# A decayed-state attention with a mixture-of-experts layer on one core: state update in one piece per head, wide scores, placed element-wise work and a new order

## The chip, the cores and the metric

The kernel runs on one NeuronCore of a Trainium2 chip. The metric is the device time of one execution in microseconds (us). The core has a TensorE for matmuls (PE; its weight loads are shown as PEld), a VectorE (DVE), a ScalarE (ACT), a GpSimd (POOL) and a SyncE (SP), which issues the DMA transfers.

## The reference

Four batches, eight heads, 768 steps, head size 48. Each step multiplies a complex state by a decay, adds the outer product of key and value, and reads it with the query. The result `x` (768 x 384 per batch) goes through four experts of attention, of which the two best are mixed per token.

```python
scale = np.minimum(mag, 0.999) / (mag + 1e-06)     # mag = |a|
for t in range(S):
    new_re = ar * S_re - ai * S_im
    new_im = ar * S_im + ai * S_re
    kv = np.einsum('bhd,bhe->bhde', k[:, :, t], v[:, :, t])
    S_re, S_im = (new_re + kv, new_im)
    y[:, :, t] = np.einsum('bhd,bhde->bhe', q[:, :, t], S_re)
...
for e in range(E):
    scores = scale * (q @ k.transpose(0, 2, 1))    # q, k, v = x @ wq[e], x @ wk[e], x @ wv[e]
    ...
    ye = a @ v @ wo[e]                             # a: causal softmax of scores
    for kk in range(K):
        mask = topk[:, :, kk] == e
        out += mask[..., None] * w[:, :, kk:kk + 1] * ye
```

## The kernel before, in words

The recurrence is worked in six chunks of 128 steps per batch. *Preparation* (`logs`, `atan`, `angles`, `sincos`, `products`) turns the decays `ab` into running magnitudes and angles and multiplies them into queries and keys (`qk`), on tiles of 128 x 768, in batch 0 in three pieces of 128 x 256. `regroup` copies these by DMA into `fm`, where each head has 96 rows (real and imaginary parts of 48).

Per chunk follow three steps. `head` transposes the keys to `kts` (bank `pk`), and makes the score product `psc` of 128 x 128 per head, which a mask turns into `pts`. It is issued in two groups of four heads; each head's 128 key columns are split into two halves of 64. `state` makes `pu`, the update of the state of 96 x 48 per head, out of `kts` and the values `vt`; the 96 rows are split into 64 and 32. VectorE adds the old state (`wst1`) and multiplies by the chunk's decay (`tst`). The last chunk of a batch has no update. `tail` adds, for each pair of heads, the product of `pts` with the values and that of the old state with the queries into `yu`, which is split into a high part `xh` and a rest `xl`.

The expert layer then projects (`proj`, bank `pp`; `vproj`, `pv`), finds row maxima (`maxpass`, `pm`), and works attention in two pairs of experts: `score` (`pss`, exponential into `pe`), `av` (`po`), `norm` (sums `dn`, weights `cb`) and `wo` (`pw`, out to `ob`). In `av` the exponentials of the later key chunks are added into the first one's tile (`SUMS`), so that `norm` needs only a few matmuls for the sums: 16 such additions per batch.

All operations are first recorded in a list (`record`), one entry per step with its engine. `ENG0` and `ENG` say for some kinds of work whether VectorE (`d`) or GpSimd (`p`) does it; the additions into `pe` (kind `sum`) and the key products stand on `p`, the other kinds on `d`. `ORDER` is a written-out order of the whole list; each engine runs its own entries in that order. `ROOMS` says which buffer each tile takes. `FILL` puts a number of dummy matmuls on the mask `keep` ahead of an entry (line 744); everything else is issued at line 752, so almost all rows of the profile carry L752 and are told apart by their tiles. Tables for ScalarE's functions are loaded at line 750.

Of the kernel before, what the change touches and what calls it, by code (L numbers as in the profile page):

```python
# [807 lines left out]
```

## Time and profile before

| what | us |
|---|---|
| median of 3 runs (526.93 to 715.49) | 529.76 |
| the profiled execution | 527.1 |
| its span, first to last instruction | 525.4 |

The profile is of one execution. An fp32 matmul shows as two records, and two weight loads. A group's busy time is the union of its records, so that for matmuls, which are pipelined, it is less than count times mean; how long a stream of them takes is read from the starts in the timeline. Waits are idle time of an engine before an instruction, with the engine that ended it.

### The profile page before, as it was taken

How to read it: one execution, taken by the hardware profiler on the slowest of the kernel's cores; microseconds unless marked ns; L12 is line 12 of the kernel's file. 1: busy time of each engine (PE TensorE's matmuls, PEld its weight loads, DVE VectorE, ACT ScalarE, POOL GpSimd, SP SyncE). 2: the span in 40 equal slices, each digit the busy share in tenths (PEclk: the TensorE clock that was granted, in tenths of full speed). 3: DMA queues.
4: the chain of work that ended last, by engine and by line, in shares of the span. 5: the costliest groups of instructions: out<-in, count | busy, mean ns of one | idle time of the engine just before them, and what ended most of it. 6: DMA issues, size and time to landing. Idle time of an engine off the chain costs nothing.

```text
span 525.4 us, 11296 instructions
## 1 busy us (share of the span) xinstructions
PE 485.1 (92%) x4546; PEld 364.4 (69%) x4546; DVE 350.0 (67%) x706; ACT 302.4 (58%) x532; POOL 179.1 (34%) x192
## 2 busy tenths in 40 slices
PE   8979999988799999999889997999899999998986
PEld 3437676766467777787567785887677878887655
DVE  4887868798964469699953686789944232647521
ACT  7897777696533777475613794856632233134453
POOL 1315050413440526341431643720425030040782
PEclk9979999989899989999997997999999998999999
DMA  8561728152370820615342702325620401010002
GB/s 294 185 201 32 207 50 257 53 171 69 88 181 18 226 85 17 200 47 153 100 141 58 210 1 75 87 72 148 181 65 21 118 2 55 17 46 30 17 1 92
DMA packets 29717, 53.52 MB, mean 102 GB/s; under 512 B 3936, under 2 KB 11616, under 8 KB 29664
## 3 DMA queue, kind: packets, MB, share of 16 engines
q1 hardware_dynamic: 29664, 52.79, 34.5%
q8 instruction: 36, 0.59, 0.5%
q14 instruction: 17, 0.14, 0.1%
HBM read 26.74 MB, written 4.72 MB: 60 GB/s over the span
## 4 chain that ended last, share of the span: by engine, by line
PE 56%; DVE 19%; ACT 13%; issue 5%; POOL 3%; DMA 3%; SPq 1%; POOLq 0%; DVEq 0%; ACTq 0%
PE pu L752 13%; PE pp L752 6%; PE psc L752 6%; PE yu L752 5%; PE pss L752 4%; DVE qk L752 4%; PE po L752 4%; DVE ab L752 4%; ACT qk L752 3%; PE pw L752 3%; PE pv L752 3%; POOL pe L752 2%; DVE junk L752 2%; ACT ab L752 2%; ACT L750 2%
## 5 line engine op out<-in xcount | busy, mean ns | idle before, releaser
L752 POOL TENSOR_TENSOR pe<-pe 128x512 f32<-128x512 f32 (+2 forms) x64 | 82.0, 1284 | 100.4 <-PE po L752 77.7
L752 PE MATMUL pu<-vt,kts 128*32 128x48 f32 (+1 forms) x640 | 75.0, 233 | 3.6 <-DVE xl L752 2.9
L752 PEld LDWEIGHTS pu<-vt,kts 128*32 128x32 f32 (+1 forms) x640 | 54.7, 125 | 24.1 <-DVE xl L752 3.4
L752 ACT ACTIVATE pe<-pss 128x512 f32<-128x512 f32 (+3 forms) x80 | 47.3, 616 | 37.9 <-PE pss L752 32.5
L752 POOL TENSOR_TENSOR qk<-qk,ab 128x256 f32<-128x256 f32 (+1 forms) x36 | 49.1, 1366 | 41.4 <-ACT ab L752 19.9
L752 PE MATMUL psc<-fm 96*64 96x128 f32 x768 | 52.3, 283 | 4.5 <-ACT kts L752 1.9
L752 PE MATMUL pss<-qka 64*128 64x256 f32 (+3 forms) x480 | 50.2, 319 | 6.2 <-ACT pe L752 4.5
L752 PEld LDWEIGHTS psc<-fm 96*64 96x64 f32 x768 | 43.0, 139 | 11.7 <-issue 2.2
L750 ACT ACT_TABLE_LOAD x39 | 50.0, 1283 | 1.4 <-PEq L797 0.8
L752 ACT ACTIVATE qk<-qk 128x256 f32<-128x256 f32 (+1 forms) x72 | 44.9, 629 | 7.5 <-DVE qk L752 6.6
L752 PEld LDWEIGHTS pss<-qka 64*128 64x128 f32 x480 | 35.6, 190 | 18.4 <-ACT pe L752 7.4
L752 POOL TENSOR_TENSOR qk<-qk 128x256 f32<-128x256 f32 (+1 forms) x18 | 20.8, 1158 | 74.1 <-ACT qk L752 45.0
L744 PEld LDWEIGHTS <-keep 128*128 128x128 bf16 x222 | 22.2, 103 | 34.0 <-issue 11.6
L752 PE MATMUL po<-pe,v 128*64 128x256 f32 (+3 forms) x320 | 45.0, 403 | 0.0
L752 POOL TENSOR_SCALAR_AFFINE_SELECT pe<-pe 128x256 f32<-128x256 f32 x48 | 22.4, 473 | 63.5 <-ACT pe L752 63.4
L752 DVE TENSOR_TENSOR pts<-psc,keep 128x512 f32<-128x512 f32 x48 | 32.5, 686 | 15.9 <-PE psc L752 15.7
L752 DVE CUSTOM_DVE_ANT_0 junk<-pm,negm 128x128 bf16<-128x128 f32 (+3 forms) x64 | 31.1, 486 | 15.7 <-PE pm L752 14.8
L752 PE MATMUL yu<-pts,vt 128*64 128x128 f32 x384 | 38.2, 288 | 1.8 <-DVE pts L752 1.0
L752 ACT ACTIVATE ab<-ab 128x256 f32<-128x256 f32 (+1 forms) x54 | 33.1, 625 | 11.5 <-DVE ab L752 11.3
L744 PE MATMUL psc<-keep 128*128 128x512 bf16 x125 | 31.1, 413 | 4.2 <-ACT kts L752 2.3
L752 ACT ACTIVATE r<-dn,col 128x512 f32<-128x512 f32 (+1 forms) x16 | 9.3, 582 | 43.8 <-PE dn L752 43.8
L752 DVE TENSOR_TENSOR qk<-qk,ab 128x256 f32<-128x256 f32 (+1 forms) x36 | 29.7, 827 | 5.3 <-ACT ab L752 4.7
(113 smaller groups left out, 987.6 us busy)
## 6 DMA issues: line engine op xcount, KB each, us to landing
fm<-qk SPq DMA_DIRECT2D x72, 192.8 KB, 3.6
qk<-in_ak_dram SPq DMA_DIRECT2D x12, 768.0 KB, 6.0
ab<-in_ak_dram SPq DMA_DIRECT2D x18, 384.0 KB, 5.2
vt<-in_vk_dram SPq DMA_DIRECT2D x12, 512.0 KB, 4.4
out_dram<-ob SPq DMA_DIRECT2D x24, 192.0 KB, 1.9
fm<-qk SPq DMA_DIRECT2D x24, 128.5 KB, 3.7
ab<-in_ak_dram SPq DMA_DIRECT2D x9, 256.0 KB, 3.6
wst<-in_w_dram SPq DMA_DIRECT2D x3, 514.0 KB, 9.3
```

What stands on the lines that cost most here:

```text
L744: nc.tensor.matmul(z, real(plan.busy), real(plan.busy)[:, None, :].to_broadcast([128, 4, 128]), start=True, stop=True)
L750: nc.scalar.preload_act_table_set(need)
L752: getattr(getattr(nc, engine), name)(*map(real, a), **{n: real(x) for n, x in k.items()})
```

## The change

- `state`: one matmul of 96 columns of weights per head, where there were one of 64 and one of 32.
- `head`: one matmul of 128 columns of weights per head, where there were two of 64.
- `tail`: three entries instead of one: the products of the first `pts`, those of the second, then all products of the state.
- Placement: `ENG0`, `ENG` and `eng` go; most element-wise work stands on VectorE or ScalarE by default, and a table `HOME` moves single entries to VectorE or GpSimd. `moved` writes an ACT entry in another engine's form. By it, of the 64 additions into `pe`, 24 stay on GpSimd and 40 go to VectorE; 52 copies and casts out of ScalarE's list go to VectorE (`xh` 10, `kts` 10, `lg` 10, `v` 7, `qka` 6, `ob` 6, `ot` 3); of the 36 scalings and absolute values of the angles, 12 stay on VectorE, 2 go to GpSimd and 22 to ScalarE; the multiplications with the decay go to GpSimd in 7 of 20 updates; and of the products in preparation GpSimd has 35 of 768 columns (27 before) and 11 of 256 (27 before).
- `logs`: the copy of the chunk ends' decay (`E`), on GpSimd before, is an ACT copy that `HOME` moves to VectorE 5 times and to GpSimd 3 times.
- `ORDER`, `ROOMS` and `FILL` are new; the dummy matmuls are 172 instead of 222.

```diff
-SUMS = ((1, 2, 3), (1, 2, 3, 4, 5))
-
-FILL = {297: 113, 299: 9, 330: 33, 363: 3, 384: 10, 409: 3, 428: 2, 437: 10, 451: 14, 465: 1, 502: 12, 504: 3, 638: 5, 966: 2, 2003: 2}
...
+HOME = {39: 'vector',
+ 47: 'vector',
...
+FILL = {293: 4, 299: 118, 301: 2, 315: 10, 318: 7, 439: 12, 462: 16, 513: 2, 2047: 1}
...
-        p.mul(eng("ratio", b, j, k0), Bi, Bi, A)
-        if eng("square", b, j, k0) == V:
-            p.act(A, Bi, AF.Square)
-        else:
-            p.mul(G, A, Bi, Bi)
+        p.mul(V, Bi, Bi, A)
+        p.act(A, Bi, AF.Square)
...
-        p.ts(eng("turns", b, j, k0), Bi, A, 0.5 / math.pi, MAGIC, OP.mult, OP.add)
+        p.act(Bi, A, AF.Copy, scale=0.5 / math.pi, bias=MAGIC)
...
-            p.mm(*((q[64 * a:64 * a + 64, i], part(b, c, 4 * g + i, 1)[:, 64 * a:64 * a + 64], part(b, c, 4 * g + i, 0), True, True)
-                   for i in range(4) for a in range(2)))
+            p.mm(*((q[:, i], part(b, c, 4 * g + i, 1), part(b, c, 4 * g + i, 0), True, True) for i in range(4)))
...
-        p.mm(*((pu[64 * a:64 * a + (64, 32)[a], h], kt[b, c][:, h, 64 * a:64 * a + (64, 32)[a]], v[:, c % 2, h, :D], True, True)
-               for h in range(H) for a in range(2)))
+        p.mm(*((pu[:, h], kt[b, c][:, h], v[:, c % 2, h, :D], True, True) for h in range(H)))
...
-            p.mul(eng("decay", 1, c, b) if b else V, t, x, e)
+            p.mul(V, t, x, e)
...
-        calls = []
-        for g in range(4):
-            for i in range(2):
-                calls.append((yu[64 * i:64 * i + 64, g], v[:, c % 2, 2 * g + i], pt[b, c, g // 2][:, 2 * (g % 2) + i], True, c == 0))
-            if c:
-                for i in range(2):
-                    calls.append((yu[64 * i:64 * i + D, g], st[b, c][:, 2 * g + i], part(b, c, 2 * g + i, 0), False, True))
-        p.mm(*calls)
+        for g in range(0, 4, 2):
+            p.mm(*((yu[64 * i:64 * i + 64, g + x], v[:, c % 2, 2 * (g + x) + i], pt[b, c, g // 2][:, 2 * x + i], c == 0 or g + x == 0, c == 0)
+                   for x in range(2) for i in range(2)))
+        if c:
+            p.mm(*((yu[64 * i:64 * i + D, g], st[b, c][:, 2 * g + i], part(b, c, 2 * g + i, 0), False, g == 3)
+                   for g in range(4) for i in range(2)))
...
-            if i in SUMS[g]:
+            if i in SUMS[b][pr][g]:
...
-                p.tt(eng("sum", 1, i, 0), y, y, x, OP.add)
+                p.tt(V, y, y, x, OP.add)
...
+def moved(engine, name, a, k):
+
+    if name != "activation":
+        return engine, name, a, k
+    o, x, f = a
+    if f == AF.Square:
+        return engine, "tensor_tensor", (o, x, x), dict(op=OP.mult)
+    if f == AF.Abs:
+        return engine, "tensor_scalar", (o.bitcast(I32), x.bitcast(I32), 0x7FFFFFFF, None), dict(op0=OP.bitwise_and, op1=OP.bypass)
+    if k:
+        return engine, "tensor_scalar", (o, x, k["scale"], k["bias"]), dict(op0=OP.mult, op1=OP.add)
+    return engine, "tensor_copy", (o, x), k
...
+            if i in HOME and HOME[i] != engine:
+                engine, name, a, k = moved(HOME[i], name, a, k)
```

TensorE's list before, at the tail of batch 0's second chunk and its state update (sizes are rows x columns of the result; the update goes on in this pattern for eight heads):

```order
L752 MATMUL psc<-fm 64x128 x8
L752 MATMUL pk<-ident,fm 128x96 x4
L752 MATMUL yu<-pts,vt 64x128 x2
L752 MATMUL yu<-fm,tst 48x128 x2
L752 MATMUL yu<-pts,vt 64x128 x2
L752 MATMUL yu<-fm,tst 48x128 x2
L752 MATMUL yu<-pts,vt 64x128 x2
L752 MATMUL yu<-fm,tst 48x128 x2
L752 MATMUL yu<-pts,vt 64x128 x2
L752 MATMUL yu<-fm,tst 48x128 x2
L752 MATMUL pu<-vt,kts 64x48
L752 MATMUL pu<-vt,kts 32x48
```

The same list of the changed kernel, some chunks of batch 0 later (`pm` is the row maximum of the expert layer):

```order
L904 MATMUL pk<-ident,fm 128x96 x4
L904 MATMUL pu<-vt,kts 96x48 x8
L904 MATMUL psc<-fm 128x128 x4
L904 MATMUL yu<-pts,vt 64x128 x8
L904 MATMUL yu<-fm,tst 48x128 x8
L904 MATMUL psc<-fm 128x128 x4
L904 MATMUL pm<-qka 128x256 x2
L904 MATMUL pu<-vt,kts 96x48 x8
L904 MATMUL yu<-pts,vt 64x128 x8
L904 MATMUL yu<-fm,tst 48x128 x8
```

An update is now eight equal matmuls of 96 rows, half a chunk's scores are four of 128, and the tail has its `pts` products together and its state products behind them; other work stands between the two halves of the scores.

GpSimd's list before, at the end of the program (additions into `pe`, and AFFINE_SELECT, the causal mask on it):

```order
L752 AFFINE_SELECT pe<-pe 128x2x128
L752 AFFINE_SELECT pe<-pe 128x256
L752 TENSOR_TENSOR pe<-pe 128x2x384
L752 TENSOR_TENSOR pe<-pe 128x2x128
L752 AFFINE_SELECT pe<-pe 128x2x128
L752 TENSOR_TENSOR pe<-pe 128x2x256
L752 TENSOR_TENSOR pe<-pe 128x512 x3
L752 AFFINE_SELECT pe<-pe 128x2x128
L752 TENSOR_TENSOR pe<-pe 128x512
L752 AFFINE_SELECT pe<-pe 128x256
L752 TENSOR_TENSOR pe<-pe 128x2x128
```

The end of VectorE's list in the changed kernel (`r` and `ot` are the normalised result and its split):

```order
L904 TENSOR_TENSOR pe<-pe 128x2x384
L904 TENSOR_TENSOR pe<-pe 128x2x128
L904 TENSOR_TENSOR pe<-pe 128x2x256
L904 TENSOR_TENSOR r<-r,cb 128x256
L904 TENSOR_TENSOR r<-r,po 128x256
L904 TENSOR_TENSOR r<-r,cb 128x512
L904 TENSOR_TENSOR r<-r,po 128x512
L904 TENSOR_TENSOR pe<-pe 128x512
L904 TENSOR_TENSOR ot_5085<-r,ot_5085 128x512
L904 TENSOR_TENSOR pe<-pe 128x512 x3
```

Of the last batch's 16 additions 14 moved from GpSimd's list to VectorE's, where they stand among the normalisation's products; two, one of 512 and one of 256, stay on GpSimd.

## Rows read from the trace of the kernel before

**Rows 1.** The head of the page and its part 1, busy time by engine.

```profile
span 525.4 us, 11296 instructions
...
PE 485.1 (92%) x4546; PEld 364.4 (69%) x4546; DVE 350.0 (67%) x706; ACT 302.4 (58%) x532; POOL 179.1 (34%) x192
```

**Rows 2.** Part 4 of the page, the chain that ended last.

```profile
PE 56%; DVE 19%; ACT 13%; issue 5%; POOL 3%; DMA 3%; SPq 1%; POOLq 0%; DVEq 0%; ACTq 0%
PE pu L752 13%; PE pp L752 6%; PE psc L752 6%; PE yu L752 5%; PE pss L752 4%; DVE qk L752 4%; PE po L752 4%; DVE ab L752 4%; ACT qk L752 3%; PE pw L752 3%; PE pv L752 3%; POOL pe L752 2%; DVE junk L752 2%; ACT ab L752 2%; ACT L750 2%
```

**Rows 3.** TensorE groups with shapes kept apart; then count | busy us, mean ns.

```profile
L752 PE MATMUL pu<-vt,kts 128*64 128x48 f32 x320 | 51.3, 243 | 3.6 <-DVE xl L752 2.9 <-ACT kts L752 0.6
...
L752 PE MATMUL pu<-vt,kts 128*32 128x48 f32 x320 | 44.8, 223 | 0.0
```

**Rows 4.** TensorE's timeline, 190 to 215: start us, length us, engine, line, records.

```profile
196.08 1.97 PE L752 MATMUL psc<-fm 96*64 96x128 f32 x32
197.88 3.60 PE L752 MATMUL pu<-vt,kts 128*64 128x48 f32 x32
201.41 0.87 PE L752 MATMUL po<-pe,v 128*64 128x384 f32 x4
...
209.16 0.52 PE L752 MATMUL pp<-xh,wlo 128*128 128x256 f32 x3
209.52 0.53 PE L752 MATMUL pp<-xl,whi 128*128 128x256 f32 x3
209.89 0.52 PE L752 MATMUL pp<-xh,whi 128*128 128x256 f32 x3
```

**Rows 5.** Weight loads by shape (rows*columns of the array).

```profile
L752 PEld LDWEIGHTS pu<-vt,kts 128*64 128x64 f32 x320 | 32.2, 139 | 15.0 <-DVE xl L752 3.4 <-ACT kts L752 1.3 <-issue 0.2
...
L752 PEld LDWEIGHTS pu<-vt,kts 128*32 128x32 f32 x320 | 22.5, 110 | 9.0
...
L752 PEld LDWEIGHTS pp<-xh,whi 128*128 128x128 f32 x144 | 20.4, 189 | 3.2 <-issue 1.0 <-ACT kts L752 0.7 <-DMA xh<-xh 0.3
```

**Rows 6.** A piece of the chain by time; loads of the dummies (page).

```profile
52.74 7.23 PE pv L744 x33
...
L744 PEld LDWEIGHTS <-keep 128*128 128x128 bf16 x222 | 22.2, 103 | 34.0 <-issue 11.6
```

**Rows 7.** Groups by shape on POOL, DVE and ACT.

```profile
L752 POOL TENSOR_TENSOR pe<-pe 128x512 f32<-128x512 f32 x40 | 53.2, 1334 | 89.6 <-PE po L752 68.1 <-ACT pe L752 19.4
...
L752 DVE TENSOR_TENSOR qk<-qk,ab 128x768 f32<-128x768 f32 x18 | 20.1, 1115 | 0.3
...
L752 POOL TENSOR_TENSOR pe<-pe 128x768 f32<-128x768 f32 x8 | 14.9, 1859 | 9.5 <-PE po L752 9.5
...
L752 ACT ACTIVATE xh<-yu 128x512 fp32r<-128x512 f32 x24 | 14.3, 596 | 28.9 <-PE yu L752 28.9
...
L752 POOL TENSOR_TENSOR pe<-pe 128x256 f32<-128x256 f32 x16 | 13.9, 872 | 1.2
...
L752 DVE TENSOR_TENSOR qk<-qk,ab 128x256 f32<-128x256 f32 x18 | 9.6, 539 | 5.0 <-ACT ab L752 4.7
...
L752 DVE TENSOR_SCALAR ab<-ab 128x768 f32<-128x768 f32 x9 | 5.2, 573 | 0.1
```

**Rows 8.** Stretches: from:to, length, busy PE, PEld, DVE, ACT, POOL (x instructions), clock.

```profile
100.00:150.00 50.00, 41.97 (x335) 30.02 (x331) 45.90 (x84) 33.11 (x49) 18.18 (x14) 0.93 0.37 104
...
484.00:517.00 33.00, 29.30 (x278) 19.36 (x276) 11.56 (x24) 17.16 (x32) 24.32 (x28) 1.00 0.06 20
```

**Rows 9.** First and last of seven POOL pieces of the chain, 488 to 515.

```profile
488.73 1.84 POOL pe L752
...
513.14 1.65 POOL pe L752 x2
```

**Rows 10.** Span and mean granted TensorE clock.

```profile
core 0: 525.4 us, clock 0.963
```

More of the change, by code (lines that the diff above doesn't have):

```diff
@@ L66 @@
-ROOMS = {'ab': [0, 1, 0, 1, 0, 1, 0, 1, 0, 1, 0, 1],
- 'carry': [0, 3, 4, 3, 5, 2],
- 'fm': [1, 0, 1, 0, 1, 0, 1, 0, 1, 0, 1, 0],
+SUMS = ((((1, 2, 3), (1, 2, 3, 4, 5)), ((1, 2, 3), (1, 2, 3, 4, 5))), (((1, 2, 3), (1, 2, 3, 4, 5)), ((1, 2, 3), (1, 2, 3, 4, 5))),
+ (((1, 2, 3), (1, 2, 3, 4, 5)), ((1, 2, 3), (1, 2, 3, 4, 5))), (((1, 2, 3), (1, 2, 3, 4, 5)), ((1, 2, 3), (1, 2, 3, 4, 5))))
+HOME = {39: 'vector',
+ 47: 'vector',
+ 54: 'vector',
+ 62: 'vector',
+ 69: 'vector',
+ 77: 'vector',
+ 86: 'vector',
+ 88: 'vector',
+ 91: 'vector',
+ 93: 'vector',
+ 96: 'vector',
+ 146: 'vector',
+ 147: 'gpsimd',
+ 161: 'gpsimd',
+ 170: 'vector',
+ 177: 'vector',
+ 180: 'vector',
+ 182: 'vector',
+ 191: 'gpsimd',
+ 193: 'gpsimd',
+ 196: 'gpsimd',
+ 199: 'gpsimd',
+ 218: 'gpsimd',
+ 233: 'gpsimd',
+ 255: 'vector',
+ 261: 'gpsimd',
+ 271: 'gpsimd',
+ 279: 'gpsimd',
+ 280: 'gpsimd',
+ 281: 'gpsimd',
+ 334: 'vector',
+ 372: 'gpsimd',
+ 388: 'gpsimd',
+ 392: 'vector',
+ 409: 'vector',
+ 443: 'gpsimd',
+ 470: 'vector',
+ 526: 'gpsimd',
+ 540: 'vector',
+ 541: 'gpsimd',
+ 554: 'gpsimd',
+ 556: 'gpsimd',
+ 564: 'gpsimd',
+ 574: 'gpsimd',
+ 590: 'gpsimd',
+ 618: 'gpsimd',
+ 626: 'gpsimd',
+ 628: 'gpsimd',
+ 636: 'gpsimd',
+ 653: 'vector',
+ 674: 'gpsimd',
+ 677: 'gpsimd',
+ 682: 'gpsimd',
+ 705: 'gpsimd',
+ 713: 'gpsimd',
+ 715: 'gpsimd',
+ 722: 'gpsimd',
+ 733: 'vector',
+ 734: 'gpsimd',
+ 736: 'gpsimd',
+ 744: 'gpsimd',
+ 747: 'gpsimd',
+ 760: 'vector',
+ 762: 'vector',
+ 783: 'gpsimd',
+ 787: 'vector',
+ 800: 'vector',
+ 801: 'vector',
+ 803: 'vector',
+ 804: 'vector',
+ 829: 'vector',
+ 831: 'vector',
+ 845: 'vector',
+ 854: 'gpsimd',
+ 871: 'vector',
+ 875: 'vector',
+ 900: 'vector',
+ 909: 'gpsimd',
+ 929: 'vector',
+ 932: 'vector',
+ 938: 'vector',
+ 992: 'gpsimd',
+ 1030: 'gpsimd',
+ 1039: 'vector',
+ 1069: 'gpsimd',
+ 1082: 'gpsimd',
+ 1092: 'gpsimd',
+ 1094: 'gpsimd',
+ 1102: 'gpsimd',
+ 1113: 'vector',
+ 1116: 'vector',
+ 1138: 'gpsimd',
+ 1140: 'gpsimd',
+ 1143: 'vector',
+ 1151: 'gpsimd',
+ 1157: 'gpsimd',
+ 1169: 'gpsimd',
+ 1180: 'gpsimd',
+ 1181: 'gpsimd',
+ 1182: 'gpsimd',
+ 1188: 'gpsimd',
+ 1199: 'gpsimd',
+ 1200: 'gpsimd',
+ 1202: 'gpsimd',
+ 1210: 'gpsimd',
+ 1211: 'gpsimd',
+ 1213: 'gpsimd',
+ 1228: 'vector',
+ 1237: 'vector',
+ 1253: 'vector',
+ 1308: 'vector',
+ 1313: 'vector',
+ 1320: 'gpsimd',
+ 1331: 'vector',
+ 1388: 'vector',
+ 1402: 'vector',
+ 1458: 'gpsimd',
+ 1473: 'gpsimd',
+ 1480: 'gpsimd',
+ 1486: 'gpsimd',
+ 1488: 'gpsimd',
+ 1496: 'gpsimd',
+ 1522: 'gpsimd',
+ 1527: 'gpsimd',
+ 1558: 'gpsimd',
+ 1560: 'gpsimd',
+ 1568: 'gpsimd',
+ 1579: 'vector',
+ 1582: 'vector',
+ 1585: 'vector',
+ 1593: 'vector',
+ 1604: 'gpsimd',
+ 1606: 'gpsimd',
+ 1609: 'vector',
+ 1623: 'gpsimd',
+ 1634: 'gpsimd',
+ 1635: 'gpsimd',
+ 1637: 'gpsimd',
+ 1645: 'gpsimd',
+ 1646: 'gpsimd',
+ 1647: 'gpsimd',
+ 1648: 'gpsimd',
+ 1666: 'gpsimd',
+ 1668: 'gpsimd',
+ 1676: 'gpsimd',
+ 1677: 'gpsimd',
+ 1678: 'gpsimd',
+ 1679: 'gpsimd',
+ 1703: 'vector',
+ 1719: 'vector',
+ 1726: 'vector',
+ 1729: 'vector',
+ 1733: 'vector',
+ 1774: 'vector',
+ 1779: 'vector',
+ 1790: 'vector',
+ 1797: 'vector',
+ 1806: 'vector',
+ 1807: 'vector',
+ 1832: 'vector',
+ 1868: 'vector',
+ 1870: 'vector',
+ 1871: 'vector',
+ 1954: 'gpsimd',
+ 1972: 'gpsimd',
+ 2026: 'gpsimd',
+ 2033: 'vector'}
@@ L69 @@
+FILL = {293: 4, 299: 118, 301: 2, 315: 10, 318: 7, 439: 12, 462: 16, 513: 2, 2047: 1}
+ROOMS = {'ab': [1, 0, 1, 0, 1, 0, 0, 1, 0, 0, 1, 0],
+ 'carry': [5, 2, 3, 0, 1, 3],
+ 'fm': [1, 0, 1, 1, 0, 1, 1, 0, 1, 0, 1, 0],
  'gcf': [0, 0, 0, 0],
@@ L384, in logs @@
         p.act(Y, X, AF.Exp)
-        p.put(G, "tensor_copy", E.rearrange("p x k c -> p k x c"),
-              Y.rearrange("p k (c t) -> p k c t", t=C)[:, :, None, :, C - 1].to_broadcast([128, k1 - k0, 2, 2]))
-        p.mul(eng("exp_q", b, j, k0), Q, Q, Y)
+        p.copy(E.rearrange("p x k c -> p k x c"),
+               Y.rearrange("p k (c t) -> p k c t", t=C)[:, :, None, :, C - 1].to_broadcast([128, k1 - k0, 2, 2]))
+        p.mul(V, Q, Q, Y)
         p.act(X, X, AF.Exp, scale=-1.0)
-        p.mul(eng("exp_k", b, j, k0), K, K, X)
+        p.mul(V, K, K, X)
     def atan(b, j, k0, k1):
@@ L415, in products @@
         A, Bi, Af, Bf, Q, K, X, Y, E = views(b, j, k0, k1)
[L416 to L419 removed]
+        p.mul(V, X, Q, Af)
+        p.mul(V, Y, K, Af)
+        p.mul(V, Q, Q, Bf)
+        p.mul(V, K, K, Bf)
     def regroup(b, k, js=(0, 1, 2)):
@@ L632, in norm @@
         dn = p.bank("dn")[:, :n]
-        left = [i for u in UNITS[g] for i in u if i not in SUMS[g]]
+        left = [i for u in UNITS[g] for i in u if i not in SUMS[b][pr][g]]
         p.mm(*((dn[64 * e:64 * e + 64, cols(g, i)[0] - t0:], onecols, pe[b, pr, g, i][:, e],
@@ L746, in attention_moe @@
         for engine, name, a, k in plan.ops[i]:
+            a, k = [real(x) for x in a], {n: real(x) for n, x in k.items()}
+            if i in HOME and HOME[i] != engine:
+                engine, name, a, k = moved(HOME[i], name, a, k)
             if name == "activation":
@@ L751, in attention_moe @@
                     table = need
-            getattr(getattr(nc, engine), name)(*map(real, a), **{n: real(x) for n, x in k.items()})
+            getattr(getattr(nc, engine), name)(*a, **k)
     last = {}
```

56 lines of the change are left out of this document (12 added, 44 removed), and 180 rows, old and new, of tables (ORDER, ROOMS).

## The prediction

> **What bounds the kernel now.** I read the busy shares first. TensorE is busy 485.1 us of a span of 525.4, VectorE 350.0, ScalarE 302.4, GpSimd 179.1 [rows 1]. A busy TensorE need not be the bound, so the chain that ended last came next: 56% of it is TensorE, 19% VectorE, 13% ScalarE, and its largest single item is the state update, `pu`, with 13% of the span, some 69 us [rows 2]. There are 20 state updates (four batches, five chunks each; the last chunk has none), so nearly every one stands on the chain at its full length. What happens in one of them is seen in TensorE's timeline: 32 records of `pu` begin at 197.88 and the next work, `po`, begins at 201.41, so eight heads take 3.53 us, 441 ns a head [rows 4]. A head has four records (each fp32 matmul shows as two), 64 columns of weights twice and 32 columns twice, with only 48 columns streaming. Beside it stands the score product: 32 records from 196.08 to 197.88, 225 ns a head for four records with 128 columns streaming [rows 4]. Work with almost three times the columns takes half the time. What differs is that the scores always alternate between two halves of 64 columns, while `pu` alternates between a width of 64 and one of 32, 320 records of each [rows 3]. So `pu` isn't paid by its columns; it is paid by changing the array's shape twice a head.
>
> **The change, part by part.**
>
> *State update in one piece.* 160 pairs of pieces (64 and 32 columns) become 160 matmuls of 96, so 640 records become 320, and no change of shape is left inside an update. The trace of before has no fp32 matmul of full width with plain weights, so I bound the cost of a record. Below: the streaming alone. The scores show 225/2 = 112 ns for 128 columns when two halves run together, so 48 columns are 42 ns and a head 84. Above: the full-width projection `pp`, whose three records take 0.36 us (209.16, 209.52, 209.89), 119 ns each with a load of 128 columns behind each [rows 4]. A head would be 238. Between them: a load takes 139 ns for 64 columns, 110 for 32 and 189 for 128 [rows 5], so 0.78 ns a column from 64 to 128, and 96 columns are 25 ns less than 128. That makes 119 - 25 = 94 ns a record and 188 ns a head. I take this, since the load is what a record of 48 columns must wait for. 160 heads: 160 x (441 - 188) = 40.5 us off; with the two ends, 57 and 32.5. All of it is on the path, by [rows 2].
>
> *Wide scores.* 768 records of 64 columns become 384 of 128. It would be a mistake to book half of 43 us here: the two halves already run side by side (two records in 112 ns). A wide record costs 112 (its streaming) to 119 (the `pp` pitch with the same load). A head is 225 to 238 against 225 now. I take the latter: 192 x 13 ns = 2.5 us more, on the path.
>
> *Split chunk ends.* The tail's product is issued as three groups instead of one, the two from `pts` first and the state's last. Number and shape of the records stay, and all have the 64-column shape: 0. It lets the second half wait alone for the second `pts`, which is part of the new order.
>
> *Element-wise work.* On GpSimd, 40 of the 64 additions of `pe` go away: 25 of 512 x 1.334, 5 of 768 x 1.859, 10 of 256 x 0.872 = 51.4 us [rows 7]. VectorE takes them; it shows no addition of 512 from SBUF, so I go between its 1115 ns for 768 and 539 for 256 [rows 7]: 827 ns, so 25 x 0.827 + 5 x 1.115 + 10 x 0.539 = 31.7 us. VectorE also takes 52 copies out of PSUM and casts from ScalarE. The longest there is `xh` with 596 ns [rows 7], so at most 31 us; most are narrower and I take 21. It gives up 24 scalings and absolute values of the angles (16 of them of 768 columns, 0.573 each: 9.2 us [rows 7]), and eight more of the 768-wide products of preparation go to GpSimd (8 x 1.115 = 9 us), while 16 of 256 come back (8.6 us). VectorE ends near 350 + 31.7 + 21 - 9.2 - 9 + 8.6 = 393 us, 82% of 480. What hides the 43 us: VectorE's idle 175 us [rows 1], and that what it gets falls into attention stages while preparation, where it is fullest (45.90 of 50 us from 100 to 150 [rows 8]), is relieved. If that cover fails, up to 43 us would be lost; if the relief in preparation reaches the chain, up to 9.2 + 9 = 18 us would be gained. I take 0 on the whole path, except at the end.
>
> *The end.* From 484 to 517 GpSimd is busy 24.32 of 33 us and VectorE 11.56 [rows 8], and the chain passes through seven pieces of POOL `pe` there, 1.84 us to 1.65, 11.0 in sum [rows 9]. In the new order 14 of the last batch's 16 additions stand on VectorE, at 827/1334 = 0.62 of the time: 11.0 x 0.38 = 4 us off. What is late next is TensorE itself.
>
> *Dummies and the new order.* Dummy matmuls (the ones on `keep`, put in where TensorE is meant to wait) fall from 222 to 172. 33 of them take 7.23 us [rows 6], so 219 ns each, 10.9 us for 50. They don't cost by themselves where TensorE waits anyway, so the bounds are 0 and 10.9; since 56% of the chain is TensorE I take about half, 5 us. For the order itself I find no row that prices it; it goes into the range.
>
> **Sum.** 525.4 - 40.5 + 2.5 - 4 - 5 = 478.4 us of span. The profiled execution took 527.1, 1.7 us more than its span, so 480. The median of the runs shown is 529.76 and the lowest 526.93; the sum is made against the profiled execution, which lies 0.5% below the median.
>
> **The rivals.**
>
> *Loads that nothing hides (slower).* The estimate rests on a load running under the record before it. If in full width each load comes before its record instead, scores pay 189 + 112 = 301 ns a record, 602 a head, and 192 x (602 - 225) = 72.4 us more, while `pu` has 164 + 42 = 206 a record, 412 a head, only 4.6 us less. 525.4 + 72.4 - 4.6 - 4 + 1.7 = 591. It decides from the point where a head's scores and update together exceed 225 + 441 = 666 ns. Against it: `pp` has a load of 189 ns and a record every 119, so its loads do overlap [rows 4, 5]. For it: `pp` is not plain fp32, and no plain fp32 of full width was seen. The Trainium skill ("TensorE: Matmul & The Clock Gate", Part 3, the mechanism) speaks for this rival: it says that weight loads overlap running matmuls only when they go to another row group, and full-width pieces all use the same rows. By that rule the time would be this rival's; the `pp` rows disagree with it, so it keeps a small chance.
>
> *VectorE takes it back.* The 43 us that VectorE gains land on the chain because its additions and copies now stand before what TensorE waits for: 480 + 43 = 523 at worst; with two thirds of it, 509. For it: 19% of the chain is VectorE already [rows 2] and its stretch from 100 to 150 is 92% full. Against: over the whole it stays at 82%, TensorE above that.
>
> *The clock falls.* The mean granted clock is 0.963 [rows 10], so TensorE ran some 39 us at its lower level (1.2 instead of 2.4 GHz), which costs about 19 us. With less TensorE work between the same waits it may idle more often and fall more often. Twice as much: 480 + 19 = 499. For it: fewer dummies. Against: the shares above leave TensorE the fullest engine.
>
> *The order gives more.* With `pu` at its lower bound (16 us more) or all of the dummies' 10.9 us, 464 to 474. For it: that fewer dummies were needed. Against: nothing shows that a wait of before goes.
>
> That the change doesn't do what it says can be left out: in the new order `pu` stands as groups of eight 96x48 and `psc` as groups of four 128x128.
>
> **How the numbers follow.** The forecast (468 to 493) has 0.57, VectorE 0.16, the clock 0.09, more gain 0.14, loads not hidden 0.04. The range holds the forecast, the clock and most of the VectorE case and of the greater gain: 460 to 510. A measurement of this kernel can tell about 2% from no change, so faster begins below 519. Of the VectorE case a tenth or two lies above that, about 0.02, and the slower rival is nearly all above 540. Faster 0.94, same 0.03, slower 0.03.
>
> **What would show it.** In the changed profile: `pu` groups of 16 records per eight heads taking about 1.5 us (right), 1.9 (by the `pp` pitch), or 3.3 (loads exposed); `psc` groups of 8 records per four heads at 0.90 to 0.95 us against 2.4; `pu` below 7% of the chain; TensorE busy near 430 us; VectorE near 390 and GpSimd near 150; the last POOL pieces of the chain gone from the end; the clock at 0.95 or more. I am wrong if `psc` shows more than 300 ns a head, if VectorE's share of the chain passes 30%, or if the saved time comes back as idle TensorE.

## The result, and the profile after

| | before | after |
|---|---|---|
| median of 4 runs each, us | 530.03 (526.93 to 715.49) | 443.63 (441.27 to 444.40) |
| the profiled execution, us | 527.1 | 443.46 |
| its span, us | 525.4 | 441.7 |

The ratio is 0.8379, 95% interval 0.8326 to 0.8432: faster by 16%. The forecast was 480 with a range of 460 to 510, so the direction was right and the gain was underrated: 36 us lie between forecast and result, and the range doesn't hold it. One execution of before took 715.49 us, and in `b_pu`, `a_prep_old`, `a_nofill` and `b_both_nofill` some executions, the profiled one among them, were disturbed: below, only the times of the others are read, and these four profiles aren't used.

The head of the page of the changed kernel, its busy times, and the chain that ended last, by engine and by line (against [rows 1, 2]):

```profile
span 441.7 us, 9807 instructions
...
PE 417.8 (95%) x3792; PEld 332.1 (75%) x3792; DVE 362.5 (82%) x772; ACT 291.0 (66%) x508; POOL 150.6 (34%) x150
...
PE 55%; ACT 16%; DVE 13%; DMA 6%; issue 4%; SPq 4%; POOL 2%; DVEq 0%; ACTq 0%; POOLq 0%
PE pss L904 8%; PE pp L904 8%; PE psc L904 7%; PE po L904 7%; PE yu L904 6%; ACT ab L904 5%; ACT qk L904 4%; ACT L902 4%; PE pu L904 4%; SPq L904 4%; PE pv L904 4%; PE pw L904 3%; DVE qk L904 3%; DVE junk L904 3%; PE pm L904 3%
```

`pu` falls from the largest item of the chain, 13%, to 4%; the chain is spread over the ordinary matmuls now. TensorE's busy time falls by 67.3 us, and its idle time as well, from 525.4 - 485.1 = 40.3 us to 441.7 - 417.8 = 23.9. The second fall is what the forecast doesn't have.

TensorE's timeline of the changed kernel in batch 1 (start us, length us, engine, line, operation, records), against [rows 4]:

```profile
163.71 1.16 PE L904 MATMUL psc<-fm 96*128 96x128 f32 x8
164.79 0.88 PE L904 MATMUL pk<-ident,fm 96*128 96x96 f32 x8
165.65 1.16 PE L904 MATMUL psc<-fm 96*128 96x128 f32 x8
166.64 1.48 PE L904 MATMUL pu<-vt,kts 128*96 128x48 f32 x16
168.06 0.62 PE L904 MATMUL pss<-qka 64*128 64x256 f32 x6
```

From start to next start, an update of eight heads takes 168.06 - 166.64 = 1.42 us, 178 ns a head (441 before, 188 forecast). Four heads' scores take 1.08 and 0.99 us, 248 to 270 ns a head (225 before, 238 forecast).

The groups of the new forms, matmuls and weight loads apart (count | busy us, mean ns of one | idle before, releasers), against [rows 3, 5, 7]:

```profile
L904 PE MATMUL psc<-fm 96*128 96x128 f32 x384 | 54.9, 289 | 5.9 <-DVE ab L904 2.0 <-DMA fm<-qk 1.8 <-ACT lg L904 1.6
...
L904 PEld LDWEIGHTS psc<-fm 96*128 96x128 f32 x384 | 48.3, 197 | 11.4 <-issue 2.3 <-DMA fm<-qk 2.1 <-DVE ab L904 2.1
...
L904 PE MATMUL pu<-vt,kts 128*96 128x48 f32 x320 | 30.0, 247 | 0.7 <-ACT kts L904 0.6
...
L904 PEld LDWEIGHTS pu<-vt,kts 128*96 128x96 f32 x320 | 28.9, 165 | 2.2 <-ACT kts L904 1.4
...
L904 POOL TENSOR_TENSOR pe<-pe 128x512 f32<-128x512 f32 x15 | 19.8, 1323 | 42.9 <-DVE pe L904 35.3 <-PE po L904 6.8 <-ACT pe L904 0.5
...
L904 DVE TENSOR_TENSOR pe<-pe 128x512 f32<-128x512 f32 x25 | 18.1, 723 | 3.4 <-PE po L904 1.8 <-POOL pe L904 0.8 <-ACT pe L904 0.3
```

320 records of `pu` instead of 640, with 30.0 us busy instead of 51.3 and 44.8. A load of 165 ns before a record every 89 ns, and one of 197 ns before a record every 124 to 135 ns, can only be if a load runs beside earlier records and loads. An addition of 512 takes 723 ns on VectorE and 1323 on GpSimd.

### A balance of TensorE

The profiles of the two kernels, and of the experiments below, can be set side by side if TensorE's span is split into four parts. *Idle* is span less busy time. *Clock* is (1 - mean granted clock) x span, what the stretches at the lower level (1.2 instead of 2.4 GHz) add. *Dummies* are their count by 219 ns [rows 6]. *Work* is what is left. The last three are estimates: they take TensorE as busy in all of the time at the lower level, and each dummy as one at the full clock. The same records take twice as long at the lower level. That is seen in the tail of before, at a low and at the full clock (windows with the granted clock in the third column from the right, then two consecutive groups of four records at each):

```profile
186.00:190.00 4.00, 4.00 (x40) 3.75 (x42) 3.47 (x5) 0.68 (x1) 0.00 (x0) 0.57 0.44 118
202.00:205.00 3.00, 3.00 (x46) 2.50 (x46) 2.32 (x7) 1.61 (x3) 2.92 (x2) 1.00 0.02 5
```

```profile
188.57 0.64 PE L752 MATMUL yu<-fm,tst 96*48 96x128 f32 x4
189.00 0.64 PE L752 MATMUL yu<-pts,vt 128*64 128x128 f32 x4
...
203.23 0.39 PE L752 MATMUL yu<-fm,tst 96*48 96x128 f32 x4
203.45 0.39 PE L752 MATMUL yu<-pts,vt 128*64 128x128 f32 x4
```

Four records go by in 0.43 us there and in 0.22 here. Of the profiled executions, in us:

| kernel | span | clock | busy | work | dummies | clock | idle |
|---|---|---|---|---|---|---|---|
| before | 525.4 | 0.963 | 485.1 | 417.1 | 48.6 | 19.4 | 40.3 |
| old order and placement, new pieces (`b_both`) | 503.9 | 0.956 | 450.5 | 379.7 | 48.6 | 22.2 | 53.4 |
| the same with new placement (`b_newplace_both`) | 503.9 | 0.958 | 448.8 | 379.0 | 48.6 | 21.2 | 55.1 |
| new order and pieces, old placement (`a_oldplace`) | 477.4 | 0.968 | 425.6 | 372.6 | 37.7 | 15.3 | 51.8 |
| new order and placement, old pieces (`a_noboth`) | 493.9 | 0.951 | 475.7 | 413.8 | 37.7 | 24.2 | 18.2 |
| after | 441.7 | 0.984 | 417.8 | 373.0 | 37.7 | 7.1 | 23.9 |

From before to after: work -44.1, dummies -10.9, clock -12.3, idle -16.4, together the 83.7 us of the span.

### The profile page after: what moved, and what is told of

Its sections match the earlier page's. It is cut to its first block, busy times and chain, and to the rows that moved or that the text cites. A ratio compares the mean times of both kernels' runs of the same rounds, so it can differ in the third digit from the quotient of the medians.

```text
span 441.7 us, 9807 instructions
## 1 busy us (share of the span) xinstructions
PE 417.8 (95%) x3792; PEld 332.1 (75%) x3792; DVE 362.5 (82%) x772; ACT 291.0 (66%) x508; POOL 150.6 (34%) x150
## 4 chain that ended last, share of the span: by engine, by line
PE 55%; ACT 16%; DVE 13%; DMA 6%; issue 4%; SPq 4%; POOL 2%; DVEq 0%; ACTq 0%; POOLq 0%
PE pss L904 8%; PE pp L904 8%; PE psc L904 7%; PE po L904 7%; PE yu L904 6%; ACT ab L904 5%; ACT qk L904 4%; ACT L902 4%; PE pu L904 4%; SPq L904 4%; PE pv L904 4%; PE pw L904 3%; DVE qk L904 3%; DVE junk L904 3%; PE pm L904 3%
## 5 line engine op out<-in xcount | busy, mean ns | idle before, releaser
L904 POOL TENSOR_TENSOR qk<-qk,ab 128x768 f32<-128x768 f32 (+1 forms) x28 | 42.4, 1526 | 66.5 <-DVE qk L904 47.4
L904 PE MATMUL psc<-fm 96*128 96x128 f32 x384 | 54.9, 289 | 5.9 <-DVE ab L904 2.0
L904 PEld LDWEIGHTS psc<-fm 96*128 96x128 f32 x384 | 48.3, 197 | 11.4 <-issue 2.3
L904 ACT ACTIVATE ab<-ab 128x768 f32<-128x768 f32 (+1 forms) x72 | 45.9, 656 | 6.5 <-DVE ab L904 3.9
L904 ACT ACTIVATE qk<-qk 128x256 f32<-128x256 f32 (+3 forms) x82 | 45.5, 575 | 6.8 <-DVE qk L904 4.4
L904 POOL TENSOR_TENSOR pe<-pe 128x512 f32<-128x512 f32 (+2 forms) x24 | 31.4, 1308 | 49.5 <-DVE pe L904 38.5
L904 POOL TENSOR_TENSOR qk<-qk 128x768 f32<-128x768 f32 (+1 forms) x18 | 27.2, 1517 | 35.7 <-ACT qk L904 17.8
L904 DVE TENSOR_TENSOR pe<-pe 128x512 f32<-128x512 f32 (+2 forms) x40 | 27.4, 684 | 4.3 <-PE po L904 2.3
L904 PE MATMUL pu<-vt,kts 128*96 128x48 f32 x320 | 30.0, 247 | 0.7 <-ACT kts L904 0.6
L904 PEld LDWEIGHTS pu<-vt,kts 128*96 128x96 f32 x320 | 28.9, 165 | 2.2 <-ACT kts L904 1.4
L904 PE MATMUL pw<-whi,ot 128*128 128x384 f32 x96 | 29.5, 354 | 0.0
```

What stands on the lines that cost most here:

```text
L904: getattr(getattr(nc, engine), name)(*a, **k)
```

## The experiments

The two matmul edits ("pieces"), the table of engines ("placement": `HOME`) and the table of order with its buffers, dummies and the split tail ("order") can be had one without the other. In the diffs `-` is the kernel that the experiment starts from: before for labels with b, after for labels with a.

### Pieces alone, in the old order

`b_pu`:

```diff
-        p.mm(*((pu[64 * a:64 * a + (64, 32)[a], h], kt[b, c][:, h, 64 * a:64 * a + (64, 32)[a]], v[:, c % 2, h, :D], True, True)
-               for h in range(H) for a in range(2)))
+        p.mm(*((pu[:, h], kt[b, c][:, h], v[:, c % 2, h, :D], True, True) for h in range(H)))
```

> The kernel before with the state update in one piece of 96 and nothing else changed (its order, placement, dummies and split scores stay). Theory 'pieces': the one-piece update frees more than its own length under any order, since TensorE then also waits less and keeps its clock; the time falls by 60 us or more, to 470 or less. Theory 'order': the update gives back its own length, 160 heads x (441 - 170) ns = 43 us at most, and the rest of what the whole change gave needs the new order or placement; 484 to 495 us.

`b_sc`:

```diff
-            p.mm(*((q[64 * a:64 * a + 64, i], part(b, c, 4 * g + i, 1)[:, 64 * a:64 * a + 64], part(b, c, 4 * g + i, 0), True, True)
-                   for i in range(4) for a in range(2)))
+            p.mm(*((q[:, i], part(b, c, 4 * g + i, 1), part(b, c, 4 * g + i, 0), True, True) for i in range(4)))
```

> The kernel before with the wide scores alone. By the sum on record +2.5 us (13 ns more for each of 192 heads); by the 112 ns that a wide record takes in the changed kernel's trace 0 (a head 224 against 225 before). Either way within 1% of before, 525 to 533 us. If the wide form matters by fewer changes of the array's shape (its neighbours pk have the full width as well), up to 5 us less.

`b_both` makes both edits:

> Old order and old placement with both new pieces (state update of 96, wide scores). If the gains of pieces, order and placement simply add, the pieces are worth the 50 us that they were under the new order: 480. If TensorE must be the fullest engine for them to count, and it isn't under the old order, they are worth what the update alone was (28 us) less what the wide scores cost alone (7): 500 to 510.

Measured: `b_pu` 497.96 (one execution), against 530.03 beside it: 32 us less, near the 'order' of its expectation (484 to 495) and far from 'pieces' (470 or less). `b_sc` 536.67, ratio 1.0142 [1.0059, 1.0225]: the wide scores cost some 7 us by themselves, which none of the expectations held. By the balance that isn't TensorE's work, which rises by 0.7 us: the mean granted clock of its profiled execution is 0.948 and the clock's price 27.8 us, against 0.963 and 19.4 (0.948 to 0.955 in its four executions, 0.951 to 0.967 in those of before beside them). `b_both` 504.64, ratio 0.9556 [0.9396, 0.9715]: 24 us less. Its page:

```profile
span 503.9 us, 9888 instructions
...
PE 450.5 (89%) x3842; PEld 349.7 (69%) x3842; DVE 351.4 (70%) x706; ACT 302.1 (60%) x532; POOL 179.5 (36%) x192
...
PE 46%; DVE 22%; ACT 11%; DMA 7%; issue 6%; POOL 5%; SPq 3%; POOLq 0%; DVEq 0%; ACTq 0%
```

By the balance, TensorE's work fell by 37.4 us, as forecast (40.5 - 2.5 = 38). The span fell by 21.5 only: idle time rose by 13.1 us, the clock's price by 2.8, and TensorE's share of the chain fell from 56% to 46%. A third of the gain became waiting for the other engines.

### Pieces undone, in the new order

`a_noboth` and `a_nosc` put the old lines back into the changed kernel, the first both of them, the second the score's alone (the diffs above with + and - exchanged).

> The changed kernel with the state update and the scores in their old pieces (64 and 32; two halves of 64). Theory 'order': the order and placement keep their gain and only the update's own length comes back, 20 x 2.16 us = 43 us, to 484 to 490 us. Theory 'pieces': order and placement give next to nothing without the shorter update; 510 us or more.

> The changed kernel with the scores in two halves of 64 again. A head takes 224 ns wide (112 a record) and 225 in halves, so by the streaming the same time, 441 to 446. By the run of the wide scores alone (+1.4% under the old order) the halves could be faster: 437 to 440. If wide scores help by saving changes of the array's shape next to pk and pu, which have the full width too (some 90 ns for each of two changes at up to 48 places, 4 to 9 us), slower: 447 to 453.

Measured: `a_noboth` 493.21, ratio 0.9316 [0.922, 0.9413], a little above the 484 to 490 of 'order', so the pieces are worth 49.6 us here. Its busy times and its chain:

```profile
PE 475.7 (96%) x4496; PEld 364.8 (74%) x4496; DVE 362.3 (73%) x772; ACT 292.0 (59%) x508; POOL 150.5 (30%) x150
...
PE 77%; ACT 10%; DVE 6%; DMA 2%; issue 2%; SPq 1%; POOL 1%; DVEq 0%; POOLq 0%; ACTq 0%
```

With 77% of the chain TensorE's, all that it saves is seen: work -40.8 us, clock -17.1, idle +5.7. `a_nosc` took 446.59 (four runs, 445.16 to 447.36), ratio 0.8424 [0.8349, 0.8499], which can't be told from 443.63. The wide scores are worth nothing that can be measured in company.

The 17 us of clock belong to the update. `a_noboth` has less idle time than any other kernel of the table, and the lowest clock (0.951 in the execution of the table, 0.958 in the other). It has two updates in a row at 369 us, TensorE is busy without a break, and the clock falls to its lower level behind them; the same two updates of after leave it at 1.00 (the updates' row of the timeline, then windows with the granted clock in the third column from the right; first `a_noboth`, then after):

```profile
369.05 8.63 PE L906 MATMUL pu<-vt,kts 128*64 128x48 f32 x64
369.00:374.00 5.00, 5.00 (x45) 3.67 (x44) 2.68 (x4) 0.50 (x1) 3.95 (x4) 0.95 0.07 20
374.00:382.00 8.00, 8.00 (x48) 6.23 (x50) 1.44 (x3) 0.60 (x1) 0.00 (x0) 0.50 0.61 142
```

```profile
334.31 2.84 PE L904 MATMUL pu<-vt,kts 128*96 128x48 f32 x32
334.00:339.00 5.00, 5.00 (x59) 4.46 (x59) 4.35 (x6) 1.20 (x2) 4.47 (x4) 1.00 0.08 22
```

Six of the nine falls of `a_noboth` come so, at or behind an update in the old pieces with TensorE busy throughout, and they hold 17.1 of its 24.2 us; the three falls of after (at 52, 103 and 120 us) come behind stretches in which TensorE waited. `a_nosc`, with the old scores and the new update, has a clock of 0.983 to 0.988. Why the old update brings the clock down, no run shows.

### Order and placement

`a_oldplace` gives every entry of the changed kernel the engine it had before; `b_newplace_both` is the changed code and its `HOME` (renumbered) with the `ORDER`, `ROOMS`, `FILL` and unsplit tail of before. `b_newplace` and `a_oldplace_noboth` are these two with the old pieces.

```diff
-HOME = {39: 'vector', 47: 'vector', ...
+HOME = {47: 'gpsimd', 50: 'gpsimd', ...
```

> The changed kernel with its order, its pieces and its dummies, but every element-wise operation on the engine it had before. Theory 'placement': the 30 us and more that the sum did not hold come from the placement (GpSimd's long additions and products no longer waited for); the time goes up to 470 or more. Theory 'order': the new order carries the gain and the placement only a little of it; 445 to 458 us.

> Old order with the new pieces and the new placement: what is left to 443.6 us is the order's (with its split chunk ends, dummies and buffers). If the parts add: 466 to 475. If the placement needs the new order: 495 or more.

> Old order and old pieces with the new placement of element-wise work. If the parts add, 34 us less, as under the new order: 496. If the other engines only matter once TensorE has become shorter, little: 518 to 530. If the placement was fitted to the new order, it may even be slower: over 530.

> The new order (with split chunk ends and dummies) alone, old pieces and old placement. If the parts add: 443.6 + 34 + 50 = 528, so the order alone gives nothing over before. If each part hides behind the other (TensorE long, so that the placement doesn't show), it lies nearer to the 493 of the new order with new placement: 495 to 510.

Medians in us, with the ratio to before for those not given yet:

| | old pieces | new pieces | worth of the pieces |
|---|---|---|---|
| old order, old placement | 528.1 to 530.0 | 504.64 | 24 |
| old order, new placement | 546.58, 1.035 [1.0175, 1.0525] | 506.34, 0.9588 [0.9431, 0.9745] | 40 |
| new order, old placement | 519.36, 0.9834 [0.9624, 1.0044] | 477.61, 0.9022 [0.8937, 0.9107] | 42 |
| new order, new placement | 493.21 | 443.63 | 50 |

The new placement costs 17 us (old pieces) or nothing that shows (new pieces) under the old order, and gives 26 and 34 us under the new one. The new order alone gives about 9 us, with an interval that reaches no change (its expectations, 528 or 495 to 510, both missed 519); with the new pieces 27, with pieces and new placement 63. Alone, no part is worth what it is worth in company. In the balance the order's 27 us (`b_both` to `a_oldplace`) are dummies -10.9, work -7.1, clock -6.9 and idle -1.6. The path from before to after, taken through the table: 530.0, 504.6, 477.6, 443.6, so pieces -25, order -27, placement -34.

The waits of TensorE (waiting line, what it waited for: us in total, times, longest), first of `a_oldplace`, then of after, tell what the placement takes away:

```profile
PE pm L738 <- DVE mx L738: 9.6, 8, 3.4
PE dn L738 <- POOL pe L738: 7.0, 6, 1.7
PE psc L738 <- DMA fm<-qk: 3.9, 1, 3.9
```

```profile
PE pv L904 <- DVE xl L904: 2.5, 1, 2.5
PE yu L904 <- DVE pts L904: 2.1, 4, 0.8
PE psc L904 <- DVE ab L904: 2.0, 1, 2.0
PE pm L904 <- DVE mx L904: 1.9, 2, 1.0
PE psc L904 <- DMA fm<-qk: 1.8, 2, 1.1
```

With the old placement TensorE's matmul of the row maxima waits for VectorE's earlier maxima (`mx`), and that of the sums (`dn`) for GpSimd's additions into `pe`. The first falls from 9.6 to 1.9 us, the second is gone. The balance agrees: from `a_oldplace` to after work stays (372.6, 373.0), and idle falls by 27.9 and clock by 8.2 us.

### Inside the placement

Each of these changes `HOME` of the changed kernel for some entries and nothing else: all 64 additions on GpSimd (`a_sums_pool`, 40 entries) or on VectorE (`a_sums_dve`, 24); the 52 copies and casts back on ScalarE (`a_copies_act`; the four of `ab` that its expectation names aren't among them); preparation's entries on the engines of before, all 99 (`a_prep_old`), the 45 of batch 0 (`a_prep0_old`), the 54 of the others (`a_prep123_old`).

```diff
 HOME = {39: 'vector',
...
+ 528: 'gpsimd',
+ 533: 'gpsimd',
...
```

> The changed kernel with all 64 additions into pe on GpSimd, as before (40 of them go back from VectorE). In the run with the whole old placement GpSimd's pe is 8% of the chain, some 38 us, against 2% for all of GpSimd in the changed kernel. Theory 'long additions': this one group carries most of the placement's 34 us; 460 to 475 us. Theory 'many small': each of the three groups carries about a third; 450 to 458.

> The changed kernel with the last 24 additions into pe on VectorE too, so none on GpSimd. GpSimd loses 31 us of work, VectorE gains some 16 and would be about 86% busy. If GpSimd's long additions still hold up the sums, 3 to 8 us less: 436 to 441. If VectorE has become the scarcer engine, slower: 446 to 455.

> The changed kernel with the 52 copies and casts (xh, kts, lg, v, qka, ob, ot and four of ab) back on ScalarE. ScalarE gets some 22 us more and VectorE some 25 less. Theory 'many small': 450 to 458 us, since ScalarE is nearly full while a batch is prepared (45.87 of 50 us from 150 to 200). Theory 'long additions': within 1% of the changed kernel, 440 to 449.

> The changed kernel with the preparation (all moved entries of qk and ab: key products of batch 0 back on GpSimd, scalings, absolute values and products of the later batches back on VectorE) as before. VectorE's share of the chain was 24% with the old placement against 13%. Theory 'many small': 450 to 458 us. Theory 'long additions': within 1%, 440 to 449. If VectorE, now 82% busy, is the bound of the preparation, over 460.

> The changed kernel with batch 0's preparation alone (45 entries of 256 columns) placed as before. Theory 'start': nothing hides the preparation of batch 0, and GpSimd's products there also stretch VectorE's (539 ns against 420 for the same 256 columns); this half carries most of what the whole preparation gave: 455 to 466 us, with the first state update at about 38.5 us instead of 35.1. Theory 'later': 444 to 450.

> The changed kernel with the preparation of batches 1 to 3 alone (54 entries) placed as before. Theory 'later': VectorE takes the scalings and products back while it is fullest (47.31 of 50 us from 150 to 200), and the next batch begins later: 456 to 466 us. Theory 'start': 444 to 450.

| kernel | us | ratio to before | against after |
|---|---|---|---|
| `a_sums_pool` | 458.77 | 0.8654 [0.8556, 0.8751] | +15 |
| `a_sums_dve` | 449.48 | 0.8535 [0.8508, 0.8563] | +6 |
| `a_copies_act` | 445.89 | 0.8411 [0.8317, 0.8504] | +2, within the scatter |
| `a_prep_old` | 468.92 (one execution) | | +25 |
| `a_prep0_old` | 447.97 | 0.8517 [0.8463, 0.8571] | +4 |
| `a_prep123_old` | 467.53 | 0.8889 [0.8845, 0.8932] | +24 |

The last column is a plain difference; by the ratios to before, taken beside each, it reads +15, +8, +2, (no ratio), +7, +27. Two moves carry the placement: the preparation of batches 1 to 3 and the additions. For the additions neither theory held in full: they carry almost half of the 34 us, not most. The 52 copies, which I had counted as VectorE's burden, are worth nothing either way, and the last 24 additions are better left on GpSimd: in `a_sums_dve` VectorE has 24% of the chain, in after 13%. The first waits of `a_sums_pool` and of `a_prep123_old` are the two that the old placement had:

```profile
PE dn L738 <- POOL pe L738: 7.7, 6, 1.6
```

```profile
PE pm L738 <- DVE mx L738: 8.3, 5, 2.9
PE pm L738 <- DVE mpart L738: 4.4, 4, 3.5
```

In `a_prep123_old` VectorE is busy 389.5 us instead of 362.5. Its stretch from 300 to 350 us and the same of after (busy PE, PEld, DVE, ACT, POOL; then the granted clock):

```profile
300.00:350.00 50.00, 44.20 (x356) 35.97 (x355) 44.46 (x99) 26.30 (x42) 18.88 (x17) 0.93 0.36 98
```

```profile
300.00:350.00 50.00, 48.77 (x474) 40.39 (x475) 34.73 (x77) 22.95 (x44) 23.89 (x21) 1.00 0.46 121
```

VectorE is fuller by 10 us of 50, and TensorE has 356 records instead of 474, at a granted clock of 0.93 instead of 1.00 (`a_prep123_old` is up to 23 us behind by then, so the two stretches don't hold quite the same work). The first state update of batch 3 shows where the time is lost, in `a_prep123_old`, `a_sums_pool` and after:

```profile
349.46 1.48 PE L738 MATMUL pu<-vt,kts 128*96 128x48 f32 x16
```

```profile
334.48 1.48 PE L738 MATMUL pu<-vt,kts 128*96 128x48 f32 x16
```

```profile
326.71 1.48 PE L904 MATMUL pu<-vt,kts 128*96 128x48 f32 x16
```

From there to the end of the span remain 114.5, 121.7 and 115.0 us. So preparation loses its 23 us wholly before batch 3, and the additions lose 7.8 before it and 6.7 behind it.

### Dummies and the split tail

`a_nofill` takes the 54 later dummies out of the changed kernel; `b_both_nofill` takes 109 out of the old order with the new pieces; `a_tail1` puts the tail's groups together again, at the place of the last of them, in 23 of 24 chunks.

```diff
-FILL = {293: 4, 299: 118, 301: 2, 315: 10, 318: 7, 439: 12, 462: 16, 513: 2, 2047: 1}
+FILL = {299: 118}
```

```diff
-FILL = {297: 113, 299: 9, 330: 33, 363: 3, 384: 10, 409: 3, 428: 2, 437: 10, 451: 14, 465: 1, 502: 12, 504: 3, 638: 5, 966: 2, 2003: 2}
+FILL = {297: 113}
```

> The changed kernel without the 54 dummies behind the first 118. If they cost their length (219 ns each), 12 us less: 431. If they stand where TensorE waits anyway, within 1%: 439 to 448. If TensorE's clock falls more often without them, slower: 448 to 460, with the granted clock below 0.98.

> The order of before with both new pieces, and of its 222 dummy matmuls only the first 113 (109 left out; nothing that the outputs need is left out). Beside it stands the same kernel with all dummies, 504.6 us, and the new order with the new pieces and the old placement, 477.6. Theory 1 (the 27 us between these two are the order's own): the dummies stand in waits, and the time stays at 500 to 510, or rises by some us if the granted clock falls below 0.956. Theory 2 (the dummies stood on the path): 109 x 0.22 = 24 us less at most; 480 to 492, and the new order's gain is then mostly that it has fewer of them.

> The changed kernel with the chunk ends in one piece again: in 23 of 24 chunks the three groups of the tail stand together where the last of them stood (in one chunk they stay apart, since a buffer of pts is written again in between). By the sum on record the split costs and gives nothing by itself: within 1%, 439 to 448 us. If the split lets TensorE work on the first pts while the second is still being masked, some 0.3 to 0.7 us (one mask of 0.69) at 23 places: 450 to 460.

Measured: `a_nofill` 443.09 to 447.98 in three executions, 0.8474 [0.8428, 0.8521], and `a_tail1` 445.05, 0.8483 [0.8402, 0.8563]: within 3 us of after by the times and some 5 by the ratios, hardly to be told from it. `b_both_nofill` 497.66 and 503.48 in two executions, 0.9497 [0.9402, 0.9591], against 0.9556 [0.9396, 0.9715] with all dummies: no difference either, where 109 x 219 ns = 24 us would have gone had they stood on the path and done nothing else. The granted clock of these two was 0.927 and 0.905, against 0.956 and 0.947 with the dummies: by the balance's estimate the clock costs 36 and 48 us there, against 22 and 27. So leaving dummies out gains nothing, but two readings of that are left. Either they stand in waits, or they cost their length and give it back by the clock that they hold up; no run tells these apart. The 27 us of the order aren't its 50 fewer dummies, since 109 fewer give nothing in the old order.

None of the versions is faster than the changed kernel.

## Why the prediction was wrong in size, step by step

- *State update, -40.5 "all of it on the path".* The size was right: 178 ns a head measured, 188 forecast, and TensorE's work fell by 37.4 (old order) to 40.8 us (new order) for both edits, 38 forecast. The mechanism, that a head pays for changes of width, is seen record by record in the trace of before (from 198 us on): two records of the same width start 67 or 94 ns apart, and two at a change of width 136 or 150 ns. After, they start 85 ns apart. "All of it on the path" was wrong for the kernel as I read it. I concluded from 13% of the chain [rows 2] that each us saved is a us gained; in the old order 13 us came back as idle time, since other engines' results then came last. It became right only with the new order and placement, and there 17 us of clock came on top.
- *Wide scores, +2.5.* 248 to 270 ns a head in the two groups shown instead of 238. By the balance TensorE's work rose by 0.7 us with them in the old order and fell by 3.0 in the new one (376.0 in `a_nosc`, 373.0 after), so the term was of the right size. The 7 us that they cost alone go into the clock by the balance, which the term didn't have; in company nothing can be told.
- *Split chunk ends, 0.* Right (`a_tail1`).
- *Element-wise work, 0 on the whole path, -4 at the end.* This is the step that failed most: -34 us in company, of which additions 15 and preparation of batches 1 to 3 24 when undone singly. I judged VectorE by its total and let its 43 us more be hidden by its 175 us of idle time; the total doesn't matter, but when VectorE is free. The relief of preparation, which I had as a bound of 18 us and then took at nothing, was the larger part: undoing it brings back TensorE's waits of `pm` for `mx`, 8.3 us instead of 1.9. For the additions I looked only at the end (-4; measured 6.7 behind the first update of batch 3), where half of their worth lies; the other half comes earlier. The total was off as well, 393 forecast and 362.5 measured: I had the additions at 31.7 us (27.3 by the groups) and the copies at 21 (24.3 for 49 of the 52), but left out scalings of 256 (3.4 us), the decay's and the result's products that leave VectorE (8 us), and that products that stay become shorter (below).
- *Dummies, -5.* 50 fewer, 10.9 us of busy time less, but leaving them out gained nothing in either order.
- *"For the order itself I find no row that prices it; it goes into the range."* This step failed too: the order was worth 27 us with the new pieces. Rows that bound it were there: 40.3 us of idle TensorE [rows 1], 48.6 us of dummies [rows 6], and 19 us of half clock [rows 10] are 108 us that are no work. The changed kernel has 68.7 left. I booked 9 (4 and 5) of the 40 that they gave.
- *The clock.* I had it only as a rival that costs 19 us. It moved the other way: 0.963 to 0.984, 12 us gained. In the old order with new pieces it was 0.956 and 0.947, beside 0.958 to 0.967 for before. It doesn't follow idle time alone: four of the eight falls of before (from 155, 186, 275 and 435 us, 8.5 of its 19.4 us) come at or behind an update in the old pieces with TensorE busy, as in `a_noboth`, and in after no such fall is left.
- *The rivals.* That nothing hides the loads (591) is refuted: by it `pu` would take 412 ns a head. The Trainium skill ("TensorE: Matmul & The Clock Gate", Part 3, the mechanism) says in its list of what overlaps that loads do so with running matmuls only on another row group, though the same section also lets a load into a background weight buffer go ahead; the loads of 165 and 197 ns in full width, with a record every 89 and 124 to 135 ns, disagree with the first sentence. That VectorE takes it back (509 to 523) is refuted: VectorE's share of the chain fell from 19% to 13%. In the old order it is partly true: of what the new placement costs there (18.2 us of span) the balance puts 8.3 into idle time and 10.5 into the clock, and in `b_newplace` TensorE's wait of `pm` for `mx` is 7.0 us, in before 2.9. "The order gives more" named the right side, with 464 to 474, and was itself too small, since it priced `pu` and dummies again instead of waits and clock.
- *What would show it.* `pu` at 1.42 us for eight heads (1.5), 4% of the chain (below 7%), TensorE busy 417.8 (near 430), GpSimd 150.6 (150), the clock 0.984 (0.95 or more) came as said; `psc` at 0.99 to 1.08 us (0.90 to 0.95) and VectorE at 362.5 (390) didn't. `pe` of GpSimd is gone from the end of the chain:

```profile
424.90 2.74 PE po L904 x24
427.64 1.12 PE pss L904 x16
428.75 2.32 PE pw L904 x12
```

What stays open: why the new placement gives nothing under the old order. `b_newplace_both` still shows 5.7 us of `pm` waiting for `mx`, and reaches batch 3's first update at 375.86 us, `b_both` at 375.56; it may be that there other entries of the in-order lists come last, but no run separates this. Open too is which waits the order takes away. Some 7 us of the order's 27 are work of TensorE by the balance, which I can't assign.

## What to carry to other kernels

Split the fullest engine's span into work, dummies, lost clock and idle time before pricing an edit: what an edit takes from the work is only gained where no other engine's result comes last, and a change of order or placement is to be priced by the other three parts, which here gave 40 of 84 us. A change of pieces can move the clock too, and here did, by 17 us in the new order. Judge an engine that gets more work by the results for which the fullest engine waits, not by its total: VectorE rose by 12.5 us, and TensorE's listed waits for it fell from 17.8 to 13.8. And undo parts within the finished version as well as adding them to the old one, since their worths don't add up: the placement cost up to 17 us in one order and gave 34 in another.
